# Constant matmuls planned into TensorE's idle time, a smaller bank reserve for the value sums, another order of the banks, gated first loads and two projections fewer

## The chip, the cores and the metric

The kernel runs on one core of a Trainium2 chip. The core has five instruction queues that run side by side: TensorE (PE) multiplies matrices, ScalarE (ACT) and VectorE (DVE) work element by element, GpSimd (POOL) does slow side work, and SyncE (SP) issues the DMAs between HBM and the on-chip memory SBUF. TensorE writes to PSUM, which has eight banks of 128 partitions x 512 float32. The metric is device time in microseconds (us), median of several runs of the whole program.

## The reference, cut to what matters

Two independent parts share one output: a spectral filter (two-dimensional FFT of `A_x`, product with complex weights, inverse FFT) and a softmax attention with 32 heads of width 20 over 2048 positions.

```python
def _A_ref(x, w_r, w_i):                       # x: 2048 x 640
    X = rfft2(x.astype(float32))
    return irfft2(X * (w_r + 1j * w_i), s=(S, D)).astype(bfloat16)

def _B_ref(x, wqkv, wo):                       # H = 32 heads, Dh = 20
    q, k, v = split(x @ wqkv)
    p = softmax(q @ k.T * Dh ** -0.5)
    return (p @ v).reshape(B, S, D) @ wo

return concatenate([a, b], axis=-1)            # 2048 x 1280
```

## The kernel before

**A planner writes the order of every queue.** The Python code does not emit instructions loop by loop. It simulates the core: `run()` advances a clock `now`, and whenever an engine is free in the simulation it asks that engine's step function for the next operation. `put()` appends the operation to the engine's list, books `occ` nanoseconds on the engine, and notes when the result will be visible to others (`vis`, the end plus a latency such as `L_PE`). `peek()` says when a set of buffers will be ready in planned time. After the simulation `emit()` writes the lists out as fixed instruction queues with semaphore waits wherever data or buffers depend on another engine. On the chip each queue runs strictly in its planned order; only the times are the chip's own.

**Attention.** The 32 heads lie in 8 groups `g` of 4, the queries in 4 chunks `qc` of 512, which makes 32 units (`UNITS`). A unit has 64 score tiles: 16 blocks of 128 keys (`kt`) for each of 4 heads (`j`). A score tile is one matmul with 32 contraction rows (`score_mm`, L776); up to four heads run side by side in the four row strips of the array. Exponentials of most tiles are made by ScalarE, two tiles (two banks) at a time (`try_exp`, L1278). The others are made by VectorE with integer tricks: one pass out of PSUM per tile (L901), then three passes over four tiles (L929, L930, L931). The product with the values, with an extra column of ones for the sums of the softmax, is `try_pv` (L1016): four heads run side by side in the column strips and accumulate into one bank per unit. When a unit is done, L1036 copies that bank out, L1048 turns it, L1055 and L1061 divide by the sums. After eight units a chunk of queries is complete, and L1083 (transpose) and L1099 (output projection) follow.

**Banks.** Banks 0 to 3 form two pairs for ScalarE (`SETS`): while one pair is read, the other is filled (`try_act_fill`). Banks 4 to 7 (`POOLB`) are shared by VectorE's score tiles, the value sums and all other matmul work. Until the first exponential is planned (`act_started` false), other work may use all eight banks, lowest number first. `ring` holds seven exponentiated pairs until the value product has read them.

**Background jobs.** All other TensorE work is cut into jobs of one bank each: transposes of `x` (L552), projections of the first two head groups (L574, `proj0`), of the other groups in packed form (L603, `packed`, 128 columns of Q or K at a time, for key chunks `kc` of 512 positions), of the values (L650), and then the four stages of the filter (L1551, L1602, L1688, L1714). `packed` results land in a staging buffer, from which `spread_heads` copies them to their heads' places by DMA; the heads of groups 0 and 1 take only positions from 1024 on, because `proj0` has made the rest.

**The order on TensorE** is decided in `step_pe`: first a fill for ScalarE if a pair of banks is free, then the rest of a job that has begun, then the value product if enough tiles wait, then a new job (`try_bg`), then a smaller value product. `room` is the planned time until ScalarE would run out of filled pairs; a job begins only if its first part fits. `try_bg` begins nothing while `want_pv()` holds, that is while exponentials of a new unit wait and no bank has been given to that unit's sums yet; the next shared bank is so kept for the sums.

**The start.** VectorE clears a buffer, TensorE runs 20 matmuls on it (`warm`, L532), and SP issues the loads in this order: identity, the first chunk of `x` in two halves, the first columns of the K and Q weights, the bias, then the second chunk of `x`, the value weights, the third and fourth chunk, the rest of the K and Q weights, and a selection matrix. POOL folds `A_x` for the filter (L1451 to L1458) between 33 and 93 us.

The filter's inputs and tables come in large loads when its stages begin; at those points TensorE has no background work until the load has landed.

Of the kernel before, what the change touches and what calls it, by code (L numbers as in the profile page):

```python
# [260 lines left out]
NU = 32  # L261
# [30 lines left out]
class KB:  # L292
# [2 lines left out]
    L_DVE = 140.0  # L295
    L_POOL = 90.0
    SW = 102.0
    FILL = 445.0
    SETS = ((0, 1), (2, 3))
    POOLB = (4, 5, 6, 7)  # L300
# [2 lines left out]
    def __init__(self, nc, A_x, A_w_r, A_w_i, B_x, B_wqkv, B_wo, out):  # L303
        self.nc = nc
        self.A_x, self.A_w_r, self.A_w_i = A_x, A_w_r, A_w_i
        self.B_x, self.B_wqkv, self.B_wo, self.out = B_x, B_wqkv, B_wo, out
        self.P = Prog()
        self.now = 0.0
        self.free = {e: 0.0 for e in ENGINES}
        self.mode = "B"  # L310
        self.switches = 0
        self.busy = {e: 0.0 for e in ENGINES}
        self.events = []
        self.jobs = []
        self.flight = []
        self.dve_q = []
        self.aux = {"sp": [], "pool": [], "act": [], "dve": []}
        self.dma_free = 0.0
        self._seq = 0
        self._str = 0  # L320
        self._gat = 0
        self.out_streams = set()
        self.bank_owner = {b: None for b in range(8)}
        self.bank_key_free = {b: 0.0 for b in range(8)}
# [79 lines left out]
    def put(self, eng, fn, occ, r=(), w=(), pw=(), name="", lat=None, mode="B"):  # L404
        t = self.P.add(eng, fn, r=r, w=w, pw=pw, name=name)
        st = self.free[eng]
        if eng == "pe" and mode != self.mode:
            st += self.SW
            self.mode = mode
            self.switches += 1  # L410
        st = max(self.now, st)
        end = st + occ
        self.free[eng] = end
        self.busy[eng] += occ
        if lat is None:
            lat = {"pe": self.L_PE, "act": self.L_ACT, "dve": self.L_DVE, "pool": self.L_POOL}[eng]
        t.vis = end + lat
        self.at(end)
        self.at(t.vis)
        return t  # L420
# [45 lines left out]
    def setup_B(self):  # L466
        cb = np.zeros((128, 256), np.float32)
        cb[:, 0:128] = np.eye(128, dtype=np.float32)
        cb[:, 128:256] = np.eye(128, dtype=np.float32) * (np.arange(128) % 32 < 20)[:, None]
        cBd = self.inline(f32_to_bf16_bits(cb), "constI")  # L470
        self.c_mask = cBd.ap()[:, 128:256]
        cf = np.zeros((128, 85 + 3), np.float32)
        for j in range(4):
            for e in range(21):
                cf[32 * j + e, 21 * j + e] = 1.0
            cf[32 * j + 20: 32 * j + 32, 85] = OFF / 12.0
            cf[32 * j + 20: 32 * j + 32, 86] = 1.0
        cf[:, 87] = 1.0
        cFd = self.nc.inline_tensor(np.ascontiguousarray(cf), "constF")
        a = self.ar  # L480
        xB = self.B_x[0].rearrange("(t p) c -> p t c", p=128)
        wv = self.B_wqkv.rearrange("(c p) n -> p c n", p=128)
        ws = self.ws
        self.dve_now(lambda e: e.memset(ws, 0.25), 600.0, w=[("ws",), ("G", 0)], name="ms_ws")
        wz = a.bf(self.zC + 8192, 2560)
        self.dve_now(lambda e: e.memset(wz.bitcast(F32), 0.0), 1200.0, w=[("w0z",)], name="ms_w0")
        self.now = 700.0
        self.warm(20)
        self.now = 0.0
        act_warm = self.ws[:, 640:648]  # L490
        self.aux["act"].append(("op", lambda e: e.activation(act_warm, ws[:, 0:8], AF.Exp), 1500.0, [("ws",), ("G", 0)], [("ws2",)], [], "act_warm", False, 0.0))
        self.dma(self.ident, cBd.ap()[:, 0:128], 32768, w=[("ident",)], name="ld_id")
        for t in range(2):
            self.dma(self.xn[0][:, 2 * t:2 * t + 2, :], xB[:, 2 * t:2 * t + 2, :], 327680, w=[("xn", 0, 2 * t), ("xn", 0, 2 * t + 1)], name="ld_x0")
        for c0, nm in ((640, "wk0"), (0, "wq0")):
            self.dma(self.wqkv[:, :, c0:c0 + 160], wv[:, :, c0:c0 + 160], 204800, w=[(nm,)], name="ld_" + nm)
        self.dma(a.f32(self.bo, 3), cFd.ap()[:, 85:88], 1536, w=[("bias",)], name="ld_bias")

        def ld_x(i):
            self.dma(self.xn[i], xB[:, 4 * i:4 * i + 4, :], 655360, w=[("xn", i, t) for t in range(4)], name="ld_x%d" % i)  # L500
        ld_x(1)
        self.dma(self.wqkv[:, :, 1280:1920], wv[:, :, 1280:1920], 819200, w=[("wv",)], name="ld_wv")
        ld_x(2)
        ld_x(3)
        self.dma(self.wqkv[:, :, 800:1280], wv[:, :, 800:1280], 614400, w=[("wk",)], name="ld_wk")
        self.dma(self.wqkv[:, :, 160:640], wv[:, :, 160:640], 614400, w=[("wq",)], name="ld_wq")
        self.dma(self.sel, cFd.ap()[:, 0:85], 43520, w=[("sel",)], name="ld_sel")
        self.dma(self.ixt, self.c_ix.ap(), 4096, w=[("ixt",)], name="ld_ix", rel=60000.0)
        for g in range(2):
            for i in (1, 0):  # L510
                d_ = self.w0[g][i].rearrange("p c (j e) -> p c j e", e=32)[:, :, :, 0:20]
                s_ = self.wqkv[:, :, 640 * i + 80 * g: 640 * i + 80 * g + 80].rearrange("p c (j e) -> p c j e", e=20)
                self.dve_push([((lambda d_, s_: lambda e, en: e.tensor_copy(d_, s_))(d_, s_), 420.0, [("w0z",), (("wq0", "wk0")[i],)], [("w0", g, i)], [], "padw")],
                              prio=0 if g == 0 else 1)
        va = self.V
        v3 = va.rearrange("p k m e -> p (k m) e")
        vo = v3[:, :, 0:168].rearrange("p a (h e) -> p a h e", e=21)[:, :, :, 20]
        one2 = float(np.uint32(0x3F803F80).view(np.float32))
        off2 = float(np.uint32(0x44A044A0).view(np.float32))
# [18 lines left out]
    def jobs_B(self):  # L538
        ps, psb = self.ps, self.psb
        J = {}  # L540
        for i in range(4):
            for t2 in range(2):
                for gi, cbs in enumerate(((0, 1, 2), (3, 4))):
                    n = len(cbs)
                    pe = []
# [72 lines left out]
        sb = 0  # L618
        hist = []
        order = [(1, 1), (0, 1), (1, 2), (0, 2), (1, 3), (0, 3), (1, 4), (0, 4), (0, 0)]  # L620
        for n_, (which, c) in enumerate(order):
                js = []
                free = hist[-2] if len(hist) >= 2 else []
                hist.append(self.spread_keys(which, c))
                for kc in range(4):
                    j = packed(which, c, kc, sb, free)
                    j.prio = 1000.0 + 10 * n_ + kc
                    j.rel = self.PJ0 + self.PJ1 * (n_ + 0.25 * kc)
                    js.append(j)
                    J[("pk", which, c, kc)] = j  # L630
# [7 lines left out]
                sb = (sb + 1) % 2  # L638
        for m in range(4):
            for k2 in range(8):  # L640
                pe = []
# [35 lines left out]
    def spread_heads(self, which, c, sb):  # L677
        dst = (self.QT, self.KT)[which]
        nm = ("QT", "KT")[which]
        for h in range(H):  # L680
            lo, hi = max(20 * h, 128 * c), min(20 * h + 20, 128 * c + 128)
            if lo >= hi:
                continue
            g, j = divmod(h, 4)
            s0 = 0
            if g < 2:
                if which == 1:
                    continue
                s0 = 1024
            d0 = 32 * j + lo - 20 * h  # L690
            o = dst[d0:d0 + hi - lo, g, s0:2048]
            i_ = self.stg[sb][lo - 128 * c: hi - 128 * c, s0:2048]
            self.dma(o, i_, (hi - lo) * (2048 - s0) * 2, r=[(nm + "m", g)] + [("stg", which, c, kc) for kc in range(4)] + [("stgb", sb, kc) for kc in range(4)] + [("z", "C", 0)],
                     w=[(nm + "h", h, c)], name="spread")

    def kq_keys(self, u, kt):
# [476 lines left out]
    def try_bg(self, room):  # L1173
        if any(J.nxt < len(J.pe) for J in self.flight):
            return False
        banks = self.POOLB if self.act_started else (0, 1, 2, 3, 4, 5, 6, 7)
        if self.act_started and (self.n_dve_banks() >= len(self.POOLB) - 1 or self.want_pv()):
            return False
        best = None
        for J in self.jobs:  # L1180
# [105 lines left out]
        return True  # L1286

    def step_pe(self):
        if self.try_act_fill():
            return True  # L1290
        nxt = sum(self.exp_occ(len(t[0])) for t in self.sets)
        limit = max(self.free["act"], self.now) + nxt - self.FILL - self.SW
        if not self.act_started or self.ua >= NU or not self.pick_set(1):
            limit = self.now + 1e9
        fin = self.ua >= NU and not self.sets
        u = self.upv
        nv = self.pv_waves(u)[1] if u < NU else 0
# [19 lines left out]
    MAXE = 0  # L1317
    MAXD = 3
    VLOW = 6

    def exp_occ(self, n):
        return 0.8333 * 512 * n + 60.0
# [615 lines left out]
```

## Time and profile before

| | us |
|---|---|
| median of 3 runs (lowest to highest) | 837.25 (836.61 to 838.1) |
| profiled execution: time, span | 841.89, 840.1 |
| PE, DVE, ACT busy in the span | 813.8, 686.3, 777.9 |
| ACT exponentials (832 x 1024 columns): busy, idle before them | 770.2, 35.5 |
| first exponential begins, last ends | 15.54, 819.76 |
| mean granted clock of TensorE | 0.957 |

The span is what the profiler recorded; 1.8 us of the profiled execution lie around it. The busy time of PE is modelled: a matmul counts until its modelled end, so that a PE that is busy 97% of the time is not at its peak. A timeline row gives start, duration, engine, line of the kernel, operation, tiles and count (neighbours of one kind are merged), and in brackets the idle time before it with what ended it. A row of the windows view gives the stretch and its length, then busy time and number of instructions of the chosen engine or line, the granted clock of TensorE (1.00 is full), the mean busy share of the DMA engines, and GB/s.

### The profile page before, as it was taken

How to read it: one execution, taken by the hardware profiler on the slowest of the kernel's cores; microseconds unless marked ns; L12 is line 12 of the kernel's file. 1: busy time of each engine (PE TensorE's matmuls, PEld its weight loads, DVE VectorE, ACT ScalarE, POOL GpSimd, SP SyncE). 2: the span in 40 equal slices, each digit the busy share in tenths (PEclk: the TensorE clock that was granted, in tenths of full speed). 3: DMA queues.
4: the chain of work that ended last, by engine and by line, in shares of the span. 5: the costliest groups of instructions: out<-in, count | busy, mean ns of one | idle time of the engine just before them, and what ended most of it. 6: DMA issues, size and time to landing. Idle time of an engine off the chain costs nothing.

```text
span 840.1 us, 15160 instructions
## 1 busy us (share of the span) xinstructions
PE 813.8 (97%) x6381; PEld 278.0 (33%) x6381; DVE 686.3 (82%) x1088; ACT 777.9 (93%) x845; POOL 95.7 (11%) x107
## 2 busy tenths in 40 slices
PE   7999999999999899999999999989999999999997
PEld 3422243332422222333323333322323333323335
DVE  3269988888888687988887899978899977878885
ACT  4579999999999889999999999999999999989991
POOL 7499500000000000000002122100000000000000
PEclk9589999999999689999999999999999999979999
DMA  8021120201111601010011111020101000010002
GB/s 293 22 90 56 43 78 1 52 2 26 27 26 26 238 1 51 21 46 17 1 52 44 37 28 28 22 93 9 51 1 50 34 1 2 1 48 16 32 33 82
DMA packets 24276, 37.38 MB, mean 44 GB/s; under 512 B 4392, under 2 KB 21546, under 8 KB 23178
## 3 DMA queue, kind: packets, MB, share of 16 engines
q1 hardware_dynamic: 23434, 35.03, 13.2%
q0 software_dynamic: 768, 1.32, 0.6%
q8 instruction: 52, 0.85, 0.4%
q14 instruction: 22, 0.18, 0.1%
HBM read 24.21 MB, written 7.86 MB: 38 GB/s over the span
## 4 chain that ended last, share of the span: by engine, by line
ACT 52%; PE 42%; DVE 5%; issue 0%
ACT arena L1278 52%; PE ps L776 14%; PE ps L1016 10%; PE ps L1714 3%; PE ps L1551 3%; PE ps L603 3%; PE ps L650 2%; PE ps L574 2%; PE ps L1048 2%; PE ps L1099 1%; DVE arena L901 1%; DVE arena L930 1%; PE ps L1602 1%; PE ps L1688 1%; PE ps L552 1%; PE ps L532 1%
## 5 line engine op out<-in xcount | busy, mean ns | idle before, releaser
L1278 ACT ACTIVATE arena<-ps 128x1024 f16<-128x1024 f32 x832 | 770.2, 1093 | 35.5 <-PE ps L776 25.1
L776 PE MATMUL ps<-arena 32*128 32x512 bf16 x2048 | 335.0, 396 | 17.3 <-ACT arena L1278 13.1
L901 DVE TENSOR_SCALAR arena<-ps 128x512 int16<-128x512 f32 x385 | 259.8, 686 | 81.8 <-PE ps L776 78.3
L1016 PE MATMUL ps<-arena 128*32 128x512 f16 x2433 | 213.4, 401 | 1.6 <-DVE arena L656 1.6
L776 PEld LDWEIGHTS ps<-arena 32*128 32x128 bf16 x2048 | 80.2, 91 | 314.4 <-ACT arena L1278 274.2
L930 DVE TENSOR_TENSOR arena<-arena 128x2048 f16<-128x2048 f16 (+1 forms) x97 | 120.9, 1246 | 1.7
L1016 PEld LDWEIGHTS ps<-arena 128*32 128x32 bf16 x2433 | 44.3, 95 | 88.4 <-issue 74.6
L929 DVE TENSOR_SCALAR arena<-arena 128x2048 uint16<-128x2048 uint16 (+1 forms) x97 | 68.2, 703 | 1.6
L931 DVE TENSOR_SCALAR arena<-arena 128x2048 uint16<-128x2048 uint16 (+1 forms) x97 | 67.4, 694 | 0.1
L1688 PE MATMUL ps<-arena 128*128 128x512 bf16 (+1 forms) x192 | 57.3, 387 | 0.0
L603 PE MATMUL ps<-arena 128*128 128x512 bf16 x180 | 52.6, 384 | 0.1
L1551 PE MATMUL ps<-arena 128*128 128x512 bf16 x160 | 48.0, 394 | 0.1
L1048 PE MATMUL ps<-arena 128*128 128x85 f32 x256 | 44.0, 297 | 0.0
L1048 PEld LDWEIGHTS ps<-arena 128*128 128x128 f32 x256 | 35.2, 198 | 14.0 <-issue 11.2
L1602 PE MATMUL ps<-arena 128*128 128x322 bf16 (+1 forms) x198 | 37.7, 303 | 0.3
L1714 PE MATMUL ps<-arena 128*128 128x320 bf16 (+1 forms) x192 | 34.4, 306 | 0.0
L650 PE MATMUL ps<-arena 128*128 128x160 bf16 x320 | 33.0, 242 | 0.0
L1633 DVE TENSOR_TENSOR arena<-ps,arena 128x644 bf16<-128x644 f32 (+1 forms) x34 | 28.0, 824 | 3.0 <-PE ps L1602 2.6
L1565 POOL COPY arena<-arena 128x5 bf16<-128x5 bf16 x1 | 0.2, 190 | 260.3 <-DVE arena L1557 260.3
L1099 PE MATMUL ps<-arena 128*128 128x320 bf16 x160 | 28.6, 301 | 0.0
L615 DVE TENSOR_SCALAR arena<-ps 128x512 bf16<-128x512 f32 x36 | 24.6, 684 | 4.7 <-PE ps L603 4.7
L650 PEld LDWEIGHTS ps<-arena 128*128 128x128 bf16 x320 | 22.4, 101 | 12.3 <-issue 10.9
(67 smaller groups left out, 416.2 us busy)
## 6 DMA issues: line engine op xcount, KB each, us to landing
arena<-ct SPq DMA_DIRECT2D x8, 1024.0 KB
out_dram<-arena SPq DMA_DIRECT2D x32, 160.0 KB
arena<-arena SPq DMA_DIRECT2D x42, 80.0 KB
arena<-in_A_x_dram SPq DMA_DIRECT2D x16, 160.0 KB
xs<-arena SPq DMA_DIRECT2D x16, 160.0 KB
arena<-xs SPq DMA_DIRECT2D x2, 1280.0 KB
arena<-in_B_x_dram SPq DMA_DIRECT2D x3, 640.0 KB
arena<-in_B_wqkv_dram SPq DMA_DIRECT2D x2, 600.0 KB
```

The source lines that it names most:

```text
L603: return lambda e: e.matmul(o, l, r_, start=(cc == 0), stop=(cc == 4))
L650: return lambda e: e.matmul(o, l, r_, start=st, stop=(c == 4), skip_group_check=True)
L776: return e.matmul(self.ps[:, bank, :], self.KT[32 * j:32 * j + 32, g, kt * 128:(kt + 1) * 128], self.QT[32 * j:32 * j + 32, g, qc * 512:(q ...
L901: return e.tensor_scalar(o, in_, 0.0, 31744.0, ALU.max, ALU.min)
L929: (lambda e, en: e.tensor_scalar(Gu, Iu, 0x3FF, 0x3800, ALU.bitwise_and, ALU.bitwise_or), 100 + 0.26 * 512 * n, ik, [("G", b), ("G2", b)], ...
L930: (lambda e, en: e.tensor_tensor(Gf, If, Gf, ALU.mult), 125 + 0.52 * 512 * n, ik + [("G", b)], [("G2", b)], [], "p3"),
L931: (lambda e, en: e.tensor_scalar(Iu, Iu, 0x7C00, 0x0008, ALU.bitwise_and, ALU.bitwise_or), 100 + 0.26 * 512 * n, [("G2", b)], ik, [], "p4"),
L1016: inst = e.matmul(self.ps[32 * j:32 * j + 32, bank, :], v_, p_, start=s_, stop=False, tile_position=(0, 32 * j), skip_group_check=True)
L1048: return lambda e: e.matmul(o, l, self.sel, start=(qt == 0), stop=(qt == 3), skip_group_check=True)
L1278: self.put("act", lambda e: e.activation(o, in_, AF.Exp, bias=ACT_BIAS, scale=ACT_SCALE), 0.8333 * 512 * n + 60.0, r=[("ps", b) for b in b ...
L1551: return lambda e: e.matmul(o, l, r_, start=(t == 0), stop=(t == 7))
L1688: return lambda e: e.matmul(o, l, r_, start=(n == 0), stop=(n == 7))
```

## The change

Five edits, in one diff:

- **Extra matmuls.** `step_pe` becomes `step_pe1`, and when that finds nothing to do, `keep_warm` may add one matmul of the identity with itself, repeated four times (128 x 128 weights, 512 columns), into the highest bank that is free in planned time. Nothing reads the result. It is added if the plan's TensorE time in the last 3413 ns is below 55%, if `room` is at least 420 ns, and if not all units are finished.
- **A model of the clock in the plan.** `put` sums planned TensorE time in windows of 3413 ns, and books double time in a window that follows one below 42%.
- **Gated loads.** The loads from the second chunk of `x` on wait for the first half of the first chunk.
- **Banks.** Until the first exponential, jobs take banks 4 to 7 first, then 0 to 3. While a new unit waits for its bank, `try_bg` may begin a job if at least two shared banks are free.
- **Two packed projections left out.** Q columns 0 to 127 for positions 0 to 1023 are no longer computed in `packed`; `spread_heads` waits only for the chunks that it copies.

```diff
+    WIN = 3413.0
+    PHASE = 0.0
+    COLD = 0.42
+    WARM = 0.55
...
         st = max(self.now, st)
+        if eng == "pe":
+            while (self.win + 1) * self.WIN + self.PHASE <= st:
+                self.cold = self.wacc.get(self.win, 0.0) < self.COLD * self.WIN
+                self.ncold += self.cold
+                self.win += 1
+            self.wacc[self.win] = self.wacc.get(self.win, 0.0) + occ
+            self.plog.append((st, occ))
+            if self.cold:
+                occ *= 2.0
         end = st + occ
...
-            self.dma(self.xn[i], xB[:, 4 * i:4 * i + 4, :], 655360, w=[("xn", i, t) for t in range(4)], name="ld_x%d" % i)
+            self.dma(self.xn[i], xB[:, 4 * i:4 * i + 4, :], 655360, r=[("xn", 0, 1)], w=[("xn", i, t) for t in range(4)], name="ld_x%d" % i)
...
-                for kc in range(4):
+                for kc in (range(2, 4) if (which, c) == (0, 0) else range(4)):
                     j = packed(which, c, kc, sb, free)
...
-        banks = self.POOLB if self.act_started else (0, 1, 2, 3, 4, 5, 6, 7)
-        if self.act_started and (self.n_dve_banks() >= len(self.POOLB) - 1 or self.want_pv()):
+        banks = self.POOLB if self.act_started else (4, 5, 6, 7, 0, 1, 2, 3)
+        if self.act_started and (self.n_dve_banks() >= len(self.POOLB) - 1 or (self.want_pv() and sum(1 for b in self.POOLB if self.bank_owner[b] is None) < 2)):
             return False
...
     def step_pe(self):
+        if self.step_pe1():
+            return True
+        return self.keep_warm()
...
+    def keep_warm(self):
+        t0 = self.now - self.WIN
+        u = 0.0
+        for st, occ in reversed(self.plog):
+            if st + occ < t0:
+                break
+            u += min(occ, st + occ - t0)
+        if u >= self.WARM * self.WIN or self.room < 216.0 + 2 * self.SW or not self.avail([("ident",)]) or self.P.peek("pe", r=[("ident",)]) > self.now:
+            return False
+        if self.ua >= NU and self.upv >= NU:
+            return False
+        fb = [b for b in range(8) if self.bank_owner[b] is None and self.P.peek("pe", w=[("ps", b)]) <= self.now]
+        if not fb:
+            return False
+        o = self.ps[:, fb[-1], :].rearrange("p (o n) -> p o n", o=4)
+        i_ = self.ident.rearrange("p (o n) -> p o n", o=1).to_broadcast([128, 4, 128])
+        self.nfill += 1
+        self.put("pe", lambda e: e.matmul(o, self.ident, i_, start=True, stop=True), 216.0, r=[("ident",)], w=[("ps", fb[-1])], name="keep")
+        return True
```

The same `r=[("xn", 0, 1)]` is added to the loads of the value weights, of the rest of the K and Q weights and of the selection matrix.

More of the change, by code (lines that the diff above doesn't have):

```diff
@@ L311, in __init__ @@
         self.switches = 0
+        self.plog = []
+        self.cold = False
+        self.win = 0
+        self.wacc = {}
+        self.ncold = 0
+        self.nfill = 0
         self.busy = {e: 0.0 for e in ENGINES}
@@ L499, in ld_x @@
         def ld_x(i):
-            self.dma(self.xn[i], xB[:, 4 * i:4 * i + 4, :], 655360, w=[("xn", i, t) for t in range(4)], name="ld_x%d" % i)
+            self.dma(self.xn[i], xB[:, 4 * i:4 * i + 4, :], 655360, r=[("xn", 0, 1)], w=[("xn", i, t) for t in range(4)], name="ld_x%d" % i)
         ld_x(1)
-        self.dma(self.wqkv[:, :, 1280:1920], wv[:, :, 1280:1920], 819200, w=[("wv",)], name="ld_wv")
+        self.dma(self.wqkv[:, :, 1280:1920], wv[:, :, 1280:1920], 819200, r=[("xn", 0, 1)], w=[("wv",)], name="ld_wv")
         ld_x(2)
         ld_x(3)
-        self.dma(self.wqkv[:, :, 800:1280], wv[:, :, 800:1280], 614400, w=[("wk",)], name="ld_wk")
-        self.dma(self.wqkv[:, :, 160:640], wv[:, :, 160:640], 614400, w=[("wq",)], name="ld_wq")
-        self.dma(self.sel, cFd.ap()[:, 0:85], 43520, w=[("sel",)], name="ld_sel")
+        self.dma(self.wqkv[:, :, 800:1280], wv[:, :, 800:1280], 614400, r=[("xn", 0, 1)], w=[("wk",)], name="ld_wk")
+        self.dma(self.wqkv[:, :, 160:640], wv[:, :, 160:640], 614400, r=[("xn", 0, 1)], w=[("wq",)], name="ld_wq")
+        self.dma(self.sel, cFd.ap()[:, 0:85], 43520, r=[("xn", 0, 1)], w=[("sel",)], name="ld_sel")
         self.dma(self.ixt, self.c_ix.ap(), 4096, w=[("ixt",)], name="ld_ix", rel=60000.0)
@@ L692, in spread_heads @@
             i_ = self.stg[sb][lo - 128 * c: hi - 128 * c, s0:2048]
-            self.dma(o, i_, (hi - lo) * (2048 - s0) * 2, r=[(nm + "m", g)] + [("stg", which, c, kc) for kc in range(4)] + [("stgb", sb, kc) for kc in range(4)] + [("z", "C", 0)],
+            self.dma(o, i_, (hi - lo) * (2048 - s0) * 2, r=[(nm + "m", g)] + [("stg", which, c, kc) for kc in range(s0 // 512, 4)] + [("stgb", sb, kc) for kc in range(s0 // 512, 4)] + [("z", "C", 0)],
                      w=[(nm + "h", h, c)], name="spread")
@@ L1288, in step_pe, with step_pe1 @@
     def step_pe(self):
+        if self.step_pe1():
+            return True
+        return self.keep_warm()
+    def step_pe1(self):
         if self.try_act_fill():
@@ L1294, in step_pe @@
             limit = self.now + 1e9
+        self.room = limit - self.now
         fin = self.ua >= NU and not self.sets
```

## The prediction, made before the changed kernel was run

> **What bounds the kernel now.** I read the page first, then the windows of ScalarE's exponentials, then TensorE in windows of 3.41 us.
>
> ```profile
> PE 813.8 (97%) x6381; PEld 278.0 (33%) x6381; DVE 686.3 (82%) x1088; ACT 777.9 (93%) x845; POOL 95.7 (11%) x107
> ...
> PEclk9589999999999689999999999999999999979999
> ...
> L1278 ACT ACTIVATE arena<-ps 128x1024 f16<-128x1024 f32 x832 | 770.2, 1093 | 35.5 <-PE ps L776 25.1
> ```
>
> ScalarE has 832 exponentials of 770.2/832 = 0.926 us each. Between the first (15.54 us) and the last (ends at 819.76) lie 804.2 us, so that 804.2 - 770.2 = 34.0 us are idle, and nearly all of it waits for the fills of L776. TensorE looks 97% busy, but its clock is not full everywhere. The exponentials alone, by stretch (busy time, count, clock, DMA):
>
> ```profile
> 15.50:42.70 27.20, 16.86 (x17) 0.56 0.23 76
> ...
> 50.00:60.00 10.00, 6.36 (x7) 0.66 0.23 68
> 60.00:100.00 40.00, 37.76 (x41) 1.00 0.14 44
> 100.00:276.00 176.00, 175.16 (x191) 1.00 0.14 33
> 276.00:299.00 23.00, 17.17 (x18) 0.55 0.60 212
> ...
> 557.00:573.00 16.00, 13.82 (x16) 0.79 0.37 132
> ...
> 745.00:760.00 15.00, 10.19 (x11) 0.54 0.07 29
> ```
>
> Length minus busy gives the idle time: 10.3, 3.6, 2.2, 0.8, 5.8, 2.2 and 4.8 us. Where the clock is 1.00, ScalarE is all but full (175.16 of 176 us; 94% in 60 to 100). 10.3 + 3.6 + 5.8 + 2.2 + 4.8 = 26.7 us of the 34.0 lie in five stretches with a clock below 1. So **the bound is ScalarE, and what it loses it loses where TensorE runs at half clock**. Such a stretch looks like this:
>
> ```profile
> 749.81 1.02 ACT L1278 ACTIVATE arena<-ps 128x1024 f16<-128x1024 f32 x1 [0.49 <-PE ps L776]
> ```
>
> At 0.926 us of work per 1.5 us or so, every exponential waits for its fill. Why does the clock fall? I cut PE's busy time in windows of 3.413 us, with an edge where the clock fell at 277.85:
>
> ```profile
> 15.03:18.44 3.41, 1.45 (x10) 1.00 1.10 384
> 25.27:28.68 3.41, 3.41 (x13) 0.50 0.00 0
> 49.16:52.57 3.41, 1.95 (x12) 1.00 0.17 48
> 274.44:277.85 3.41, 2.11 (x18) 1.00 0.23 54
> 438.28:441.69 3.41, 2.52 (x29) 1.00 0.17 44
> 554.33:557.74 3.41, 2.14 (x20) 1.00 0.00 0
> 564.57:567.98 3.41, 2.16 (x17) 1.00 0.74 291
> 742.06:745.47 3.41, 1.96 (x16) 1.00 0.63 232
> ```
>
> The six full-clock windows in which PE is busy 1.45 to 2.16 us are the ones behind which the clock falls to 0.50; the lowest that keeps it has 2.52. So the limit lies between 2.16 and 2.52 of 3.41 us. Once down, a window busy throughout (25.27) doesn't bring it back: the falls last 7, 2, 6, 1, 1 and 4 windows. And a low window isn't one long gap:
>
> ```profile
> 742.97 0.39 PE L776 MATMUL ps<-arena 32*128 32x512 bf16 x3
> ...
> 744.81 0.39 PE L776 MATMUL ps<-arena 32*128 32x512 bf16 x3 [0.53 <-ACT arena L1278]
> ```
>
> The filter waits for a load here, and PE has only fills, at 742.97, 743.89 and 744.81, with 0.53 us idle before the last two.
>
> **The change part by part.** *Extra matmuls in the gaps (276, 557, 745).* The missing busy time is at most 2.52 - 1.96 = 0.56 us in the last row above, 0.41 at 274.44, 0.38 at 554.33: one or two matmuls of this length.
>
> ```profile
> 59.99 0.39 PE L574 MATMUL ps<-arena 128*128 128x512 bf16 x1
> 741.26 0.39 PE L776 MATMUL ps<-arena 32*128 32x512 bf16 x2
> 741.57 0.14 PEld L1688 LDWEIGHTS ps<-arena 128*65 128x65 bf16 x2 [0.23 <-issue]
> 741.58 0.62 PE L1688 MATMUL ps<-arena 128*65 128x512 bf16 x2
> 742.13 0.39 PE L776 MATMUL ps<-arena 32*128 32x512 bf16 x2
> ```
>
> An added matmul has L574's form: 0.39 us, with up to 0.23 for the switch of weights before it; 0.53 us of idle time hold one. The plan asks for 0.55 x 3413/216 = 8.7 passes of 216 ns per window; the 742.06 window has some five (four fills, one value product), so several are added, if one of four shared banks is free. If the clock stays, 5.8 + 2.2 + 4.8 = 12.8 us of idle time go. I take three quarters, **-9.5 us** (ends -12.8 and 0), since the plan's idle time and the chip's need not lie at the same place.
>
> [...]
>
> *The start.* The first pair of fills is late for want of a bank:
>
> ```profile
> 11.85 0.75 DVE L582 TENSOR_SCALAR arena<-ps,arena 128x512 bf16<-128x512 f32 x1 [0.33 <-PE ps L574]
> ...
> 14.35 0.49 DVE L656 CAST arena<-ps 128x320 bf16<-128x320 f32 x1 [0.95 <-PE ps L650]
> ...
> 15.11 0.09 PEld L776 LDWEIGHTS ps<-arena 32*128 32x128 bf16 x2 [0.42 <-DVE arena L656]
> ...
> 15.54 1.02 ACT L1278 ACTIVATE arena<-ps 128x1024 f16<-128x1024 f32 x1 [1.45 <-PE ps L776]
> ...
> 19.63 0.62 PE L1016 MATMUL ps<-arena 128*32 128x512 f16 x4
> ```
>
> Its operands are ready at 11.85 + 0.75 = 12.60, but it waits for the copy of a value projection out of bank 0 or 1. With banks 4 to 7 used first it can start near 12.9, and the exponential 0.43 later, at 13.3 instead of 15.54: at most -2.2. I take **-2.0** (other end 0).
>
> Then, from 15.5 to the first value product at 19.63, the old reserve lets no job begin, though seven are ready (K and Q of group 1 for two chunks, Q of group 0 for the second, two value jobs; five of them alone are 25 x 0.233 = 5.8 us by the row of L574 below). That is how window 15.03 got to 1.45. The new reserve lets them run, and fills come on top: 2.52 - 1.45 = 1.07 us are wanted. If the clock stays, ScalarE should lose what it loses in 60 to 100, 2.24/40 = 5.6% or 1.5 us, instead of 10.3: at most -8.8. I take two thirds, **-6.0** (other end 0), as one low window costs the stretch.
>
> [...]
>
> *50 to 60 us.* The fall at 52.57 has another origin:
>
> ```profile
> 48.37 2.31 DVE L930 TENSOR_TENSOR arena<-arena 128x2048 f16<-128x2048 f16 x1
> ...
> 52.67 1.04 PE L1016 MATMUL ps<-arena 128*32 128x512 f16 x8 [1.56 <-DVE arena L656]
> ...
> 269.22 1.22 DVE L930 TENSOR_TENSOR arena<-arena 128x2048 f16<-128x2048 f16 x1
> ```
>
> While POOL folds, L930 takes 2.31 us instead of 1.22; VectorE runs late, and PE stands 1.56 us in front of a bank. The plan doesn't know it, and a fill planned behind would wait too. I take **0** (ends -3.6 and +3.6, the present loss gone or met twice).
>
> *Gated loads.*
>
> ```profile
> 1.15 1.01 SPq L440 DMA_DIRECT2D arena<-in_B_x_dram  x2
> ...
> 3.95 0.43 SPq L440 DMA_DIRECT2D arena<-in_B_x_dram  x1
> ...
> 7.53 1.28 PE L552 MATMUL ps<-arena 128*128 128x128 bf16 x20
> ...
> 11.65 1.28 PE L552 MATMUL ps<-arena 128*128 128x128 bf16 x20
> ```
>
> SP will stand in front of the issue of 3.95 until the first half has landed, before 7.53, and with it everything behind: value weights, chunks three and four, the other weights, later the loads of the fold. The first chunk isn't waited for now (PE goes from the 20 first matmuls straight on), so nothing is won. The second chunk is issued at up to 7.5 and takes at most what the first takes, 7.53 - 1.15 = 6.4 us: 13.9, against its use at 11.65. Loss 0 to 2.3; I take **+0.3**, as half a chunk should land well before 7.5.
>
> *Two projections and the reserve.*
>
> ```profile
> 9.48 2.33 PE L574 MATMUL ps<-arena 128*128 128x512 bf16 x10 [0.68 <-ACT arena L558]
> ...
> 820.00:841.00 21.00, 8.11 (x55) 1.00 0.24 82
> ```
>
> Ten matmuls are 2.33 us. Background work is never finished early: 8.11 us of the filter's last stage (second row, L1714 alone) run after the last exponential, on the path to the end. What is saved earlier comes off there: at most -2.3 for the projections, I take **-1.0**, because the filter still waits for its loads in between. Two copies out of PSUM go too, on a VectorE that is 82% busy: nothing. The reserve also opens PE at the 31 later unit changes: up to the other 5.8 us of the 8.11, or as much the other way if a job in front of a value product holds up the ring of seven pairs. I take **-0.5**.
>
> *Fills where none are needed.* Where jobs run, the plan is mostly over 55%. If some hundred fills fall there, most into idle time: between 0 and 0.62 us each (0.39 + 0.23). I take **+1.2**, two full ones.
>
> Sum: -9.5 - 2.0 - 6.0 + 0 + 0.3 - 1.0 - 0.5 + 1.2 = -17.5. The profiled execution took 841.89 (span 840.1), so 824.4 profiled; the median lies 4.64 below the profiled run, and 837.25 - 17.5 = **819.8**.
>
> **The rivals.** [...]
>
> *B: the fills do not hold the clock*, because none finds a free bank, or because the clock answers to something else. For it: VectorE takes up to three shared banks and the sums one. Against it: six of six falls follow a low window. Then 9.5 and 6.0 go, and the 1.2 with them: 837.25 - 2.0 + 0.3 - 1.0 - 0.5 = 834.
>
> *C, on the other side: the fills stand in front of fills for ScalarE.* In the rows at 741.26 a period is 0.87 us, PE busy throughout; a constant matmul planned there as 216 ns takes 0.39 + 0.23, or waits for a bank that a late VectorE still reads. At half of 0.62, 0.3 us each, the gain of 17.5 is gone from 58 such fills on; ninety make 837.25 + 27 - 17.5 = 846.8. For it: nobody measures the idle time on the chip, and in 60 to 100 VectorE is late. Against it: `room` of 420 ns leaves 200 ns behind a fill, and fills are asked for only below 55%.
>
> **How the numbers follow.** Forecast 0.44, A 0.22, B 0.13, C 0.18, and 0.03 for more than the forecast's range, with nearly all ends together (801 to 808). The predicted time is 819.8. 808 to 835 holds forecast, A and B, 0.79. A difference of 0.2% (1.7 us) is about what a measurement of this kernel can tell from none. Faster: 0.44 + 0.22 + 0.03 + 0.08 of B = 0.77. Same: 0.05 of B and 0.04 of C = 0.09. Slower: 0.14.
>
> **What would show it.** Mean clock above 0.98 instead of 0.957, with 1.00 in 276 to 299 and 745 to 760; first exponential near 13.3; 26 to 30 of them before 42.7 instead of 16.86/0.926 = 18; a new line of 128x512 matmuls, some tens to two hundred; fewer than 55 matmuls of L1714 behind the last exponential. I am wrong if the clock is full and ScalarE idles behind L776 all the same (C), if the clock stays near 0.957 (B), or if the number of exponentials moves by more than ten (9 us), which nothing here predicts.

## The result, and the profile after

| | before | after |
|---|---|---|
| median (lowest to highest), us | 837.41 (836.61 to 838.1) | 811.15 (810.81 to 811.51) |
| ratio, 95% interval | | 0.9687 (0.967 to 0.9704) |
| profiled execution: time, span, us | 841.89, 840.1 | 811.1, 809.3 |
| mean granted clock | 0.957 | 1.00 |
| first exponential begins, last ends, us | 15.54, 819.75 | 15.11, 790.99 |
| extra matmuls | none | 11 |

The change is 26.3 us (3.1%) faster; 819.8 was predicted, with a range of 808 to 835. A median below may hold executions that its comparison leaves out as disturbed, so that the ratio counts where the two differ.

The page of the changed kernel, in the same parts as the page of before (busy time, the 40 slices with the clock, the group of the exponentials, now at line 1297):

```profile
PE 787.8 (97%) x6382; PEld 271.0 (33%) x6382; DVE 686.2 (85%) x1085; ACT 774.3 (96%) x846; POOL 98.0 (12%) x107
...
PEclk9999999999999999999999999999999999999999
...
L1297 ACT ACTIVATE arena<-ps 128x1024 f16<-128x1024 f32 x832 | 766.1, 1093 | 10.0 <-PE ps L1035 4.7
```

The clock row has no dip left. ScalarE still has 832 exponentials, and VectorE still has its 385 tiles; the idle time before them has gone from 35.5 to 10.0 us. Of that 4.7 wait for the value product and 4.5 for the fills of L795, where 25.1 waited for the fills before. By stretch, as before (busy time, count, clock, DMA):

```profile
15.00:42.70 27.70, 27.08 (x30) 1.00 0.31 103
42.70:50.00 7.30, 6.11 (x7) 1.00 0.34 107
50.00:60.00 10.00, 9.20 (x11) 1.00 0.29 85
60.00:100.00 40.00, 37.75 (x41) 1.00 0.17 49
...
250.00:290.00 40.00, 40.00 (x44) 1.00 0.36 125
...
500.00:560.00 60.00, 57.60 (x64) 1.00 0.14 45
...
700.00:760.00 60.00, 59.56 (x66) 1.00 0.11 38
```

Up to 42.7 us there are 30 exponentials in place of 17, and the filter's first load (259 to 270 us here) costs ScalarE nothing: 40.00 of 40 us. The only large loss left after 100 us is one wait of 1.74 us for the value product, near 509.

The change's own matmuls are one group, in the view of all groups:

```profile
L1363 PE MATMUL ps<-arena 128*128 128x512 bf16 x11 | 3.8, 387 | 0.0
```

Eleven of them, 3.8 us in all. They stand in three clusters, at 257 to 261, near 530 and at 710 to 711 us, each just before or at one of the filter's loads. TensorE at the last of these:

```profile
708.88 0.39 PE L795 MATMUL ps<-arena 32*128 32x512 bf16 x2 [0.35 <-ACT arena L1297]
709.80 0.39 PE L795 MATMUL ps<-arena 32*128 32x512 bf16 x2 [0.53 <-ACT arena L1297]
710.12 0.40 PE L1035 MATMUL ps<-arena 128*32 128x512 f16 x4
710.45 0.39 PE L1363 MATMUL ps<-arena 128*128 128x512 bf16 x1
710.77 0.39 PE L795 MATMUL ps<-arena 32*128 32x512 bf16 x3
711.10 0.61 PE L1363 MATMUL ps<-arena 128*128 128x512 bf16 x2
```

The gaps of 0.53 us in front of a fill are the ones that the kernel before had from 743 on; here three of the extra matmuls stand in the next ones, and the fills behind them (710.77) show no idle time before them. In the first 250 us there is not one extra matmul: whatever repaired the start was something else.

**Where the 30.8 us between the two spans went:** idle time between first and last exponential 34.0 to 9.8 (-24.2); the exponentials' own busy time 770.2 to 766.1 (-4.1); behind the last one 20.35 to 18.31 (-2.0); first exponential 15.54 to 15.11 (-0.4).

The four executions of the changed kernel have mean clocks of 0.999 to 1.00. Of all stretches of 3.41 us between 9 and 780 us, wherever one lays them, this one has the least work of TensorE, 2.53 us, where the windows behind which the clock of the kernel before fell have 1.45 to 2.18 us:

```profile
706.40:709.81 3.41, 2.53 (x29) 1.00 0.63 230
```

### The profile page after: what moved, and what is told of

The parts are those of the page before. It is cut to its first block, busy times and chain, and to the rows that moved or that the text cites. A ratio compares the mean times of both kernels' runs of the same rounds, so it can differ in the third digit from the quotient of the medians.

```text
span 809.3 us, 15164 instructions
## 1 busy us (share of the span) xinstructions
PE 787.8 (97%) x6382; PEld 271.0 (33%) x6382; DVE 686.2 (85%) x1085; ACT 774.3 (96%) x846; POOL 98.0 (12%) x107
## 3 DMA queue, kind: packets, MB, share of 16 engines
q1 hardware_dynamic: 23434, 35.03, 13.7%
## 4 chain that ended last, share of the span: by engine, by line
ACT 50%; PE 43%; DVE 5%; issue 0%; DMA 0%; DVEq 0%
ACT arena L1297 50%; PE ps L795 15%; PE ps L1035 9%; PE ps L1759 4%; PE ps L669 3%; PE ps L1733 2%; PE ps L622 2%; PE ps L1647 2%; PE ps L1067 2%; PE ps L1118 1%; PE ps L593 1%; DVE arena L920 1%; DVE arena L949 1%; PE ps L1596 1%; PE ps L551 1%; DVE arena L948 1%
## 5 line engine op out<-in xcount | busy, mean ns | idle before, releaser
L1297 ACT ACTIVATE arena<-ps 128x1024 f16<-128x1024 f32 x832 | 766.1, 1093 | 10.0 <-PE ps L1035 4.7
L795 PE MATMUL ps<-arena 32*128 32x512 bf16 x2048 | 326.2, 384 | 10.5 <-ACT arena L1297 7.6
L1035 PE MATMUL ps<-arena 128*32 128x512 f16 x2433 | 202.8, 385 | 0.9 <-DVE arena L675 0.4
L795 PEld LDWEIGHTS ps<-arena 32*128 32x128 bf16 x2048 | 80.0, 91 | 297.4 <-ACT arena L1297 273.5
L949 DVE TENSOR_TENSOR arena<-arena 128x2048 f16<-128x2048 f16 (+1 forms) x97 | 120.0, 1237 | 2.0
L948 DVE TENSOR_SCALAR arena<-arena 128x2048 uint16<-128x2048 uint16 (+1 forms) x97 | 69.8, 719 | 1.7
L950 DVE TENSOR_SCALAR arena<-arena 128x2048 uint16<-128x2048 uint16 (+1 forms) x97 | 67.5, 696 | 0.0
L622 PE MATMUL ps<-arena 128*128 128x512 bf16 x170 | 49.3, 383 | 0.2
L1596 PE MATMUL ps<-arena 128*128 128x512 bf16 x160 | 47.2, 384 | 0.0
L1067 PEld LDWEIGHTS ps<-arena 128*128 128x128 f32 x256 | 33.3, 190 | 14.3 <-issue 11.8
L669 PEld LDWEIGHTS ps<-arena 128*128 128x128 bf16 x320 | 21.3, 98 | 12.4 <-issue 10.1
```

Source lines behind the costliest of these rows:

```text
L622: return lambda e: e.matmul(o, l, r_, start=(cc == 0), stop=(cc == 4))
L669: return lambda e: e.matmul(o, l, r_, start=st, stop=(c == 4), skip_group_check=True)
L795: return e.matmul(self.ps[:, bank, :], self.KT[32 * j:32 * j + 32, g, kt * 128:(kt + 1) * 128], self.QT[32 * j:32 * j + 32, g, qc * 512:(q ...
L948: (lambda e, en: e.tensor_scalar(Gu, Iu, 0x3FF, 0x3800, ALU.bitwise_and, ALU.bitwise_or), 100 + 0.26 * 512 * n, ik, [("G", b), ("G2", b)], ...
L949: (lambda e, en: e.tensor_tensor(Gf, If, Gf, ALU.mult), 125 + 0.52 * 512 * n, ik + [("G", b)], [("G2", b)], [], "p3"),
L950: (lambda e, en: e.tensor_scalar(Iu, Iu, 0x7C00, 0x0008, ALU.bitwise_and, ALU.bitwise_or), 100 + 0.26 * 512 * n, [("G2", b)], ik, [], "p4"),
```

## Experiments

Twelve kernels ran. W is my theory, read from the six falls of the kernel before: the clock falls behind a window of some 3.4 us in which TensorE has too little work (there 1.45 to 2.18 us). One part of the change has no run: the clock model in the plan. In the plan of the changed kernel it doubles one window only, behind the last exponential, and without it the planner writes the same order for TensorE up to the tail.

**1. The same order, without the eleven matmuls.** Their waits stay in the queue.

```diff
+                if t.name == "keep":
+                    return
                 inst = t.fn(eng)
```

> The changed kernel with its order and all its waits kept, but the eleven extra matmuls not emitted; nothing of the result is left out, since nothing reads them. Theory W (work per window): the clock falls behind any window of about 3.4 us in which TensorE is busy less than some 2.2 to 2.5 us, and the eleven matmuls are what keeps three windows above that. Then the clock falls near 258 to 262, 530 and 710 us, and the idle time of before comes back there (5.8, 2.2 and 4.8 us in that kernel): 811.2 + 8 to 13 = 819 to 824 us, mean clock 0.96 to 0.98. Rival G (order alone): the new order has taken the low windows away and the eleven matmuls do nothing: 810.5 to 811.5 us, clock 1.00.

Measured: 821.64 us, ratio 0.9824 (0.9756 to 0.9892), clock 0.983 in the profiled execution. The exponentials' group, and TensorE in the windows that end where the clock falls:

```profile
L1299 ACT ACTIVATE arena<-ps 128x1024 f16<-128x1024 f32 x832 | 767.9, 1091 | 17.3 <-PE ps L797 11.7
```

```profile
259.45:262.86 3.41, 2.31 (x22) 1.00 0.73 196
532.51:535.92 3.41, 2.40 (x19) 1.00 0.00 0
716.83:720.24 3.41, 2.06 (x22) 1.00 0.47 194
```

Three falls, at the three clusters and nowhere else before 819 us, behind windows with 2.31, 2.40 and 2.06 us of work; they last 17.1, 6.8 and 3.4 us. ScalarE's idle time after 100 us is 12.4 us, against 5.0 in the changed kernel. So **3.8 us of matmuls whose result nobody reads are worth 10.5 us** (821.64 - 811.15). W holds, G falls; my rival B falls too.

**2. Transposes in place of the matmuls**, four of 128 columns each, at the same places.

```diff
-        self.put("pe", lambda e: e.matmul(o, self.ident, i_, start=True, stop=True), 216.0, ...)
+        for q in range(4):
+            inst = e.transpose(self.psb[:, bk, q * 128:(q + 1) * 128], self.ident, self.ident)
```

> The changed kernel with each extra matmul replaced by four transposes of the identity (the same 512 columns, at the same eleven places). If transposes count for the clock as matmuls do: as the changed kernel, 810.5 to 812 us, clock 1.00. [...]

Measured: 811.77 us, ratio 0.9679 (0.9633 to 0.9724), clock 0.999.

```profile
L1368 PE MATMUL ps<-arena 128*128 128x128 bf16 x44 | 3.8, 221 | 0.0
```

44 transposes, 3.8 us as well. At a mean clock of 0.999 the profiled execution (span 808.6 us) was at half clock for less than 2.5 us in all, less than one window; the other three have 0.998. Without the eleven matmuls it was 0.970 to 0.983 in four executions, and 821.64 us (run 1). So here the eleven groups of four hold the clock as the matmuls do.

**3. The extra matmuls as the only change** to the kernel before.

```diff
     def step_pe(self):
+        if self.step_pe1():
+            return True
+        return self.keep_warm()
...
```

> The kernel before with the extra matmuls as its only change (the plan places eleven, two of them between the first exponential and the first value product). Theory W: the three gaps of the filter hold the clock, worth up to 12.8 us; the window at 15 to 18.4 us wants 1.07 us of busy time more, and two matmuls are 0.6 to 0.8, so the start still falls: 837.4 - 10 to 13 = 824 to 827 us. If two are enough for the start: 815 to 818. If the fills are worth nothing: 837.

Measured: 825.55 us (four executions: 823.51, 823.73, 827.37 and 839.16), ratio 0.9841 (0.9773 to 0.991), as W has it. Windows of TensorE at the start and at the first load:

```profile
17.39:20.80 3.41, 1.89 (x14) 1.00 0.70 242
...
37.87:41.28 3.41, 3.41 (x18) 0.50 0.16 53
...
269.97:273.38 3.41, 2.46 (x17) 1.00 0.22 53
```

No fall from 42 to 819 us, but the start falls at 20.8, behind a window with 1.89 us, and stays down for six windows: two matmuls were too few for it. At the load a window with 2.46 us holds.

**4. Reserve and bank order together, no extra matmul.**

```diff
-        banks = ... (0, 1, 2, 3, 4, 5, 6, 7)
-        if ... or self.want_pv()):
+        banks = ... (4, 5, 6, 7, 0, 1, 2, 3)
+        if ... or (self.want_pv() and sum(1 for b in self.POOLB if self.bank_owner[b] is None) < 2)):
```

> The kernel before with the smaller reserve for the value sums and banks 4 to 7 used first, and nothing else (no extra matmul). Theory W: the jobs that now run between 15 and 20 us keep the start at full clock (10 us of idle time less before 42.7 us, and some of the 3.6 us between 50 and 60), the three gaps fall as before: 837.4 - 10 to 13 = 824 to 827 us. Rival: it is the gated loads that repaired the start, and this one stays at 835 to 838.

Measured: 816.8 us, ratio 0.9736 (0.969 to 0.9782): better than W's 824 to 827. The start is at full clock (27.34 us of exponentials up to 42.7, 27.08 in the changed kernel), and the gaps fall, as expected; but they fall for less (6.8, 13.7 and 3.4 us at 272, 528 and 716, before 20.5, twice 3.4 and 13.7), and only 14 matmuls of the last stage are left behind the last exponential, where the kernel before has 56.

**5. Each of the two alone.**

> The kernel before with only the smaller reserve for the value sums. Reserve and banks together took 816.8 us and kept the start at full clock. If the reserve is what fills TensorE between 15 and 20 us (my theory): start at full clock, 817 to 820 us, first exponential still near 15.5 or later. If the order of the banks does it: the start falls as before, 832 to 838.

> The kernel before with only banks 4 to 7 used first until the first exponential. By my theory the fill is earlier (first exponential up to 1 us earlier than in the kernel before) but the jobs behind it stay locked out, the window at 15 to 18 us stays low, the clock falls at the start: 835 to 838 us. If the bank order does it alone (both pairs filled at once, so that ScalarE and the jobs flow): 817 to 822.

Measured: reserve alone 838.36 (ten executions), ratio 1.002 (0.9993 to 1.0048), no gain at all. Banks alone: four executions of 830.09, 833.41, 847.74 and 848.35 us at mean clocks of 0.974, 0.968, 0.942 and 0.942, no interval. In both profiled executions (834.76 and 833.41) the start is at full clock, which I had expected of the reserve only. The start with the banks alone (TensorE):

```profile
14.91 0.39 PE L776 MATMUL ps<-arena 32*128 32x512 bf16 x4
15.24 0.59 PE L650 MATMUL ps<-arena 128*128 128x160 bf16 x6
16.42 0.39 PE L776 MATMUL ps<-arena 32*128 32x512 bf16 x2 [0.59 <-ACT arena L1278]
17.34 0.39 PE L776 MATMUL ps<-arena 32*128 32x512 bf16 x2 [0.53 <-ACT arena L1278]
18.25 0.39 PE L776 MATMUL ps<-arena 32*128 32x512 bf16 x2 [0.53 <-ACT arena L1278]
```

It has the same gaps as before. Of all stretches of 3.41 us that begin between 12 and 20 us, these have the least work of TensorE: in the kernel before, with the banks alone, with the reserve alone, and with both (run 4):

```profile
15.70:19.11 3.41, 0.92 (x9) 0.91 1.08 378
```

```profile
14.85:18.26 3.41, 1.76 (x18) 1.00 1.09 382
```

```profile
15.90:19.31 3.41, 2.45 (x27) 1.00 1.07 377
```

```profile
15.25:18.66 3.41, 3.24 (x28) 1.00 1.09 380
```

So the reserve does most to fill the start. With the banks alone the clock holds in the profiled start in spite of a stretch with 1.76 us; laid on the edges at which the clock of this execution changes later (266.46 us and on), its two windows there, from 13.87 and from 17.28, have 2.35 and 2.83 us. That this is what spared the start is my reading, which no run tests. Whether the start fell in its executions at 0.942 isn't shown, as they have no trace. What the reserve wins at the start it mostly gives back in the profiled execution: a later first exponential (16.64 us), falls at 478 to 492 and 566 to 581 us, and a longer tail. The filter's last stage behind the last exponential, before, after, with the reserve alone, and (from run 8) in the changed kernel with the old bank order:

```profile
819.75:840.10 20.35, 8.36 (x56) 1.00 0.25 85
```

```profile
790.99:809.30 18.31, 2.48 (x16) 0.98 0.17 57
```

```profile
806.75:832.90 26.15, 13.28 (x90) 1.00 0.23 79
```

```profile
796.31:828.20 31.89, 19.10 (x134) 0.98 0.25 86
```

56, 16, 90 and 134 of 192 matmuls remain, and the tail is 20.35, 18.31, 26.15 and 31.89 us. So a changed bank rule acts far from where it was put, by way of the order of the later jobs.

**6. The loads not gated.**

```diff
-            self.dma(self.xn[i], ..., r=[("xn", 0, 1)], w=...)
+            self.dma(self.xn[i], ..., w=...)
```

> The changed kernel with the loads not gated; the planned order of TensorE, VectorE, ScalarE and SP is the same, only waits of SP are gone. My term for the gate was +0.3 us (0 to 2.3): 810.5 to 811.2 us. If the gate helps by giving the first chunk the DMA engines for itself: slower, 812 to 814.

Measured: 810.81 us, ratio 0.9696 (0.9668 to 0.9725): the gate neither helps nor hurts by more than the spread. In the changed kernel SP passed it at 4.29 us, where it had issued that load at 3.95.

**7. An extra matmul wherever one fits**, 34 of them.

```diff
-    WARM = 0.55
+    WARM = 2.0
```

> The changed kernel with the limit of 55% raised to 200%, so that every place where the plan has idle time, room and a bank gets an extra matmul (34 instead of 11). My rival C: each stands in front of a fill at 0.3 us: 811.2 + 23 x 0.3 = 818 us. If the room of 420 ns keeps them out of the way: 810.5 to 812 us, and ScalarE's idle time stays near 10 us.

Measured: 811.46 us, ratio 0.9705 (0.9677 to 0.9733).

```profile
L1363 PE MATMUL ps<-arena 128*128 128x512 bf16 x34 | 11.0, 385 | 0.0
```

Three times as many, and ScalarE's idle time stays at 10.0 us. My rival C falls: with `room` of 420 ns none stands in a fill's way. It also says how rarely the plan sees idle time, room and a bank together: 34 times in 800 us.

**8. The changed kernel with one edit undone**: the old reserve, the old bank order, or the two projections back.

> The changed kernel with the old, larger reserve for the value sums (the plan then places 17 extra matmuls, two of them between the first exponentials). The kernel before with the banks alone fell at the start in some executions and not in others. Theory W: the two matmuls there bring 0.6 to 0.8 us to a window that holds about 1.9 with the banks alone, which is at the limit of 2.4: 811 to 816 us, clock at or near 1.00 from 100 us on. If the reserve is needed: falls at the start, 821 to 826.

> The changed kernel with the banks before the first exponential taken from 0 upwards as before. From the start of the run with the reserve alone (first exponential 16.64, start at full clock, longer tail) and the fills in the gaps: first exponential 1 to 1.5 us later, clock near 1.00, 812 to 817 us; if the order of the jobs toward the end suffers as with the reserve alone (tail 26 instead of 18 us): 818 to 822.

> The changed kernel with the two unread projections computed again. My term was -1.0 us for leaving them out (0 to -2.3): 811.5 to 813.5 us, clock 1.00, more matmuls of the filter's last stage behind the last exponential. If they were hidden: 810.5 to 811.5.

Measured: without the reserve 816.83, ratio 0.9747 (0.9719 to 0.9776); without the bank order 832.68, ratio 0.9948 (0.9927 to 0.9968); with the projections 814.15, ratio 0.9714 (0.9689 to 0.974). Without the reserve it is just above my 811 to 816; the start holds in the profiled execution, and what costs is something else: the plan gives ScalarE 836 exponentials in place of 832 (769.7 us of work in place of 766.1), and the tail is 1.6 us longer, with a fall at 798.6.

The bank order, for which I had 2 us, is the dearest to undo: 21.5 us, above both of my ranges. Between the two profiled executions it is 19.0 us, of which 13.6 are tail (31.89 - 18.31), and the clock falls at 86, 468 and 581 us in spite of twelve extra matmuls, none of which stands between 300 and 490 us. A part of this is the clock model's and not the banks': with the old bank order it doubles eight windows of the plan, and the same planner without it leaves 84 matmuls behind the last exponential and not 134. By the tails of run 5 that would be some 7 us of the 13.6, an estimate that no run tests.

With the projections, four executions took 810.97, 813.79, 814.52 and 820.12 us at mean clocks of 0.999, 0.996, 0.996 and 0.984: in the one at full clock the projections cost nothing (810.97), and the rest goes with the clock. In the profiled one (820.12) an extra matmul comes too late:

```profile
261.21 0.39 PE L795 MATMUL ps<-arena 32*128 32x512 bf16 x3 [0.20 <-ACT arena L1297]
262.13 0.39 PE L795 MATMUL ps<-arena 32*128 32x512 bf16 x3 [0.53 <-ACT arena L1297]
262.45 0.40 PE L1035 MATMUL ps<-arena 128*32 128x512 f16 x4
262.78 0.51 PE L1363 MATMUL ps<-arena 128*128 128x512 bf16 x1
```

```profile
259.51:262.92 3.41, 2.62 (x21) 1.00 0.05 12
262.92:266.33 3.41, 3.41 (x17) 0.50 0.22 53
```

The clock falls at 262.92. The extra matmul begins at 262.78, so that only 0.14 us of it lie in the thin window. The plan looks 3413 ns back from its own now; that a full stretch at the beginning of that time hid the thin one behind it is my reading, which no run tests.

**9. Three output buffers and 16 first matmuls.** The tail of the changed kernel waits 1.16 us for a store, and its first 20 matmuls run until 8.53 us.

```diff
-        self.outB = [a.bf(a.take(1280), 640) for _ in range(2)]
+        self.outB = [a.bf(a.take(1280), 640) for _ in range(3)]
-        self.warm(20)
+        self.warm(16)
...
```

> The changed kernel with three output row buffers instead of two (in its tail the last projection waits 1.16 us for a store that still reads one) and 16 instead of 20 matmuls on the cleared buffer at the start (the first half of x had landed by 4.29 us, when SP passed its gate, and TensorE is still at these matmuls until 8.5). Expected: -1.0 for the buffer, -0.9 to -1.7 for the four matmuls: 808.5 to 809.5 us. [...] If the plan's order shifts against it: 811 to 813.

Measured: 812.95 us, ratio 0.9714 (0.9698 to 0.9729): no gain. The first exponential is at 14.33 instead of 15.11, but then (ScalarE's timeline):

```profile
14.33 6.52 ACT L1297 ACTIVATE arena<-ps 128x1024 f16<-128x1024 f32 x7 [0.82 <-PE ps L795]
25.57 4.69 ACT L1297 ACTIVATE arena<-ps 128x1024 f16<-128x1024 f32 x5 [4.72 <-PE ps L1035]
```

Seven exponentials fill the ring of seven pairs by 20.85, and ScalarE stands 4.72 us before the first value product (24.49): the plan, started earlier, has put 20 matmuls of the projection of the values at 21.92, where the changed kernel has them before 15.6. No version beat the changed kernel by more than the spread.

## Why the prediction was right, and which sizes were off

**What bounds the kernel: right.** ScalarE's idle time sat where the clock was down, and falls follow thin windows; run 1 shows it by taking 3.8 us of work away and nothing else, with three falls behind windows of 2.06 to 2.40 us. The prediction's windows were laid 0.07 us early (the clock fell at 277.92 and not at 277.85); on the right edges its six have 1.45 to 2.18 us, which changes nothing.

**Gaps at the loads (-9.5):** idle time after 100 us went from 17.6 to 5.0 (34.0 and 9.8 less what lies before 100: 16.4 and 4.75), -12.6. The mechanism is as predicted, but not all of this is the extra matmuls': without them the changed kernel has 12.4 us (run 1), so that 7.4 are theirs and 5.2 the new order's. In the old order (run 3, 6.9 us left) they take 10.8. The -9.5 lies between the two. No long gap is needed: in the window that ends with the fall at 745.54 the waits for a fill are 0.53 us each, and its work is 1.89 us; without the eleven matmuls the clock fell at the three loads, and with them it holds (run 1). In these traces every fall before the end of the work follows a window with 2.62 of 3.41 us or less.

**The start (-2.0 and -6.0):** the first exponential moved by 0.4 only, because the first 20 matmuls took 6.92 instead of 6.08 us; from their end to it, 7.85 became 6.58, -1.3. From 15.5 to 42.7 the idle time went from 10.3 to 0.5, -9.8, beyond my outer bound of -8.8: that bound took the loss at full clock from 60 to 100 us (5.6%), where VectorE is late, and at the start it is 1.8%. Part of it comes back as 1.0 us more idle time in 42.7 to 50.

**How the start was held: right but for the extra matmuls.** I gave the merit to the reserve, with extra matmuls on top. There are no extra ones in the start of the changed kernel. The rows of run 5 give the reserve the larger part (0.92 to 2.45 us in the thinnest stretch) and the bank order the rest (3.24 with both); run 4 shows that together they leave the start at full clock. That the start would fall to half clock all the same had a chance of 0.22 (A); in the changed kernel the clock is 1.00 from 15.00 to 42.70.

**50 to 60 us (0):** -2.8. VectorE's L930 (now L949) still takes up to 2.30 us while POOL folds, but in the new order no window gets thin there: no stretch of 3.41 us that begins between 45 and 60 us has less than 2.92 us of work.

**Tail (-1.0 and -0.5):** -2.0 in sum, but not by my reasoning: the projections are worth nothing at full clock (one execution, run 8), and the reserve alone lengthens the tail by 5.8 us. The sign of the reserve's part was wrong taken alone; the order of the banks turns it.

**Not foreseen: -4.1** in the busy time of the exponentials. One that stands alone takes 1.02 us (749.81 before), seven in a row take 6.52 (14.33 in run 9), 0.92 for each after the first. The difference is saved wherever a wait has gone; there were 60 breaks between exponentials, and 30 are left. That makes some 3 us, an estimate from these rows.

**Gate (+0.3), fills in the way (+1.2):** both nothing, runs 6 and 7. The sign that I had named, some tens to two hundred extra matmuls, failed too: there are eleven.

The largest error of the step by step sum is the bank order. Its price in the sum was the first exponential, 2 us; undone in the finished change it costs 21.5, with the clock model's share in it (run 8). The forecast was 8.7 us too high; two parts that it had at nothing, 50 to 60 us and the exponentials' own time, are 2.8 and 4.1, and that the total stayed inside the range is owed to the range's width as well. The edits do not add up: 10.5 for the matmuls, 5.7 for the reserve, 21.5 for the banks and 3.0 for the projections make 40.7, against 26.3 in all. Besides, 4.5 of the 30.8 us between the two profiled executions are the profiled one of before being longer than its median.

**What stays open:** why the plan's jobs advance faster with the new bank order. By the issue of the filter's last table 741 exponentials have begun in the changed kernel, 754 in the one before, 776 with the reserve alone and 797 in the changed kernel with the old bank order, and the tail follows that number. Between the last two the clock model makes most of the difference in the plan (84 or 134 matmuls left, run 8); which of the planner's choices makes the others was not tried.

## What to carry to other kernels

Where a profile shows that an engine that isn't the bound loses its clock, look for thin windows and not only for long gaps: cut its busy time into windows that end where the clock falls, and compare those that fall with those that hold. Here eleven matmuls without any use, 3.8 us, were worth 10.5 us (run 1), nearly three times their own time; they stand in time that was idle, and one that began 0.14 us before the end of its window was too late (run 8). In a kernel whose order a planner writes, price an edit by its experiment and not by its place: the smaller reserve gave nothing alone and, together with the bank order, 21 us.

## What the runs showed of the hardware that was not expected

- In the busy time that the trace models the limit isn't sharp. The 27 falls before the end of the work, in all fourteen traces, follow windows with 1.45 to 2.62 of 3.41 us (2.62 in run 8). But a window with 2.46 held the clock (run 3), one with 2.35 too (13.87 with the banks alone), and behind the last exponential of the changed kernel even one with 2.08 (795.14 to 798.56).
- In each trace with several changes of the clock these lie whole multiples of 3.413 us apart (before: 18.51, 42.40, 52.64, 59.47 and 277.92, which is 7, 3, 2 and 64 of them). Where these edges lie, counted from the start of the span, differs from trace to trace: 18.51 in the kernel before is 1.44 us behind a multiple of 3.413, 272.26 in run 4 is 2.61. That one kernel can fall or not for this reason is my reading: no kernel has two traces. What was measured is that the kernel before took 835.01 us at a mean clock of 0.969 and 837.72 at 0.962 in two executions beside run 8, and that run 8's projections spread over 9 us, while the changed kernel's four executions lie within 0.7 us.
- Once down, the clock stayed down for up to six or seven windows though TensorE is busy for 2.88 to 3.41 us in each (20.80 to 41.28 in run 3, 18.51 to 42.40 before), so that one thin window cost anything from 3.4 to 24 us of half clock. What decides is open.
- Four transposes of 128 columns in place of each matmul of 512 hold the clock as the matmuls do: 811.77 us at 0.998 to 0.999, against 811.15 at 0.999 to 1.00 (run 2).
